# Alternating GpSimd's gathers with its table steps in an FFT-plus-ReGLU kernel

## The chip, the cores and the metric

The kernel runs on one core of one Trainium2 chip. Its time is the device time of one execution in microseconds; the number that counts is the median of the runs. The profile is of one execution, taken by the hardware profiler.

## The reference

The input x holds 8 batches of 3008 rows by 256 columns. Every batch goes through a two-dimensional FFT, of which the real part is kept; the rows that come out go through a gated feed-forward layer with 1536 inner columns.

```python
def _attn_ref(x):
    X = np.fft.fft(x, axis=1)
    X = np.fft.fft(X, axis=2)
    return X.real.astype(np.float32)

def _moe_ref(x, w_gate, w_val, w_out):
    gate = np.maximum(x @ w_gate, 0.0)
    val = x @ w_val
    return (gate * val @ w_out).astype(np.float32)

# x: (8, 3008, 256); w_gate, w_val: (256, 1536); w_out: (1536, 256)
# reference(x, ...) = _moe_ref(_attn_ref(x) as 24064 rows of 256, ...)
```

## The kernel before

**The transform.** The column transform is folded into the weights: the matrices `WA` and `WB` are the gate and value weights already multiplied by the cosine and sine tables `TA` and `TB`. The row transform is made with matmuls against two sets of tables, `tabC` and `tabS`, of which the odd columns are made during the set-up and the even columns later (below). Symmetries of the input halve and halve again the work: the rows of a batch (`XD`) and the same rows in mirrored order (`XG`) are added and subtracted ("folds"), most of it on GpSimd.

**Order of work.** The schedule is written out by hand. Each engine executes its own instructions in the order in which the program issues them, and waits on semaphores for the others. TensorE has the matmuls, ScalarE the ReLU of the gate (L814) and copies out of PSUM, VectorE the products of gate and value (`h`, L823), GpSimd the folds; SP issues most DMAs, GpSimd some.

**Batch 0** is done in four blocks (`segments`) of 376 or 377 columns, each of 12 tiles `fi`. A tile takes two gate matmuls, a ReLU, a third gate matmul (L804, the mirror half) and a second ReLU in the same PSUM bank, and the same three matmuls for the value, with two products on VectorE. The bank of the gate is one of two. Between them stand the matmuls of the second layer (L710). In the lists `more[(block, fi)]` stand steps that are slipped into a tile: the remaining weights (L380, L384) in the first eight tiles of block 0, and the steps of the even tables from tile 8 of block 0 on.

**The even tables.** For each of six columns `c` of `even_order`, `even_turns` (L430, L431) makes on GpSimd the whole number of turns of each angle, rounded, into a slice of the spare buffer `AA`. Later VectorE subtracts it from the angle (L455, `u` times `kvec` minus the slice), ScalarE takes the sine of it (L456), VectorE its absolute value (L457), and ScalarE the cosine (L458). The starting places of the six columns, counted in tiles, are

```python
EVEN_AT = (8, 10, 12, 14, 16, 17)
```

**The masking step.** Column 5 of `u`, one number per partition, is set to zero from partition 120 on. It is the lambda `u5` (L751), a VectorE instruction on 128x1 numbers that stands in tile 5 of block 0. Only L455 of column 5, the third in `even_order`, needs it; the odd tables use the copy `us`, masked in the set-up (L334).

**GpSimd's list around the change** is the function `turns_and_rows`. Ahead of it GpSimd has made the even-family folds of batch 0 (L439 to L443). Then come the turns of the six columns, with one step `minus_v` (L474, a product into the mirror operand `CB` of block 1) after the fourth, and after the turns six gathers (`load_mirror`, L117): indirect DMAs issued by GpSimd, each of which brings 128 or 120 mirrored rows of batch 1, 2 KB each, into `XG`. The next step of GpSimd is the fold of batch 1 (L150), which waits for a token `go` that VectorE writes in tile 6 of block 1 (L756) and for the gathers to land. On SP's queue the same function issues the rows of batch 1 (L94, L99, L102) and `reverse(2)` (L132), a copy of batch 2 in reversed row order from HBM to HBM.

**Later batches** are done in three blocks of 512 columns, with the sum of two parts made by L949 and L950 on VectorE and GpSimd.

Of the kernel before, what the change touches and what calls it, by code (L numbers as in the profile page):

```python
# [15 lines left out]
ALU = mybir.AluOpType  # L16
# [18 lines left out]
def kernel(  # L35
# [8 lines left out]
    nc = tc.nc  # L44
# [18 lines left out]
    def single(name, shape, dt=F32, pool=const):  # L63
        return pool.tile(shape, dt, name=name, tag=name)
# [26 lines left out]
    def load_rows(b, ts=range(3)):  # L91
        for t in ts:
            n = (128, 128, 120)[t]
            nc.sync.dma_start(out=XD[0:n, :, t].rearrange("p r a d -> p r (a d)"),  # L94
                              in_=dram(x, (b * S + 1 + t * 256) * D, [[2 * D, n], [H * D, 2], [1, 2 * D]]))

    def load_row_0(b):
        for r in range(2):
            nc.sync.dma_start(out=XD[120:121, r, 2], in_=dram(x, (b * S + r * H) * D, [[0, 1], [0, 2], [1, D]]))  # L99

    def load_mirror_0(b):
        nc.sync.dma_start(out=XG[120:121, :, 2, :, :].rearrange("p r a d -> p r (a d)"), in_=dram(x, b * S * D, [[H * D, 2], [1, 2 * D]]))  # L102
# [12 lines left out]
    def load_mirror(b, t, r):  # L115
        n = (128, 128, 120)[t]
        nc.gpsimd.indirect_dma_start(  # L117
            out=XG[0:n, r, t, :, :].rearrange("p a d -> p (a d)"), out_offset=None, in_=pairs,
            in_offset=bass.IndirectOffsetOnAxis(ap=gidx[0:n, 2 * t + r:2 * t + r + 1], axis=0), element_offset=b * S * D)
# [8 lines left out]
    def reverse(b):  # L128

        for r in range(2):  # L130
            top = (H - 1 - r * (H // 2)) - NC * PC + PC
            nc.sync.dma_start(out=xr[b, 1 - r], in_=dram(x, b * S * D + top * 2 * D, [[PC * 2 * D, NC], [-2 * D, PC], [1, 2 * D]]))  # L132
# [96 lines left out]
    pidx = single("pidx", [128, 1])  # L229
    back = single("back", [128, 1])  # L230
    u = single("u", [128, 6])
# [111 lines left out]
    nc.vector.tensor_scalar(wv[:], pidx[:], scalar1=119.0, op0=ALU.is_lt, scalar2=0.5, op1=ALU.mult)  # L343
    nc.vector.tensor_scalar(wv[:], wv[:], scalar1=0.5, op0=ALU.add, scalar2=None)

    upright = []

    def turn(r):
# [24 lines left out]
    def weights(c):  # L373

        f = slice(c * 512, (c + 1) * 512)

        def one(i, T, W):
            p = psO.tile([128, 512], F32, name="o", tag="o")
            for kc in range(2):
                nc.tensor.matmul(p[:], lhsT=T[:, kc, :], rhs=wr[i][c][:, kc, :], start=(kc == 0), stop=(kc == 1))  # L380
            if (i, c, W) == (0, 1, WA):
                return lambda: nc.scalar.copy(W[i][:, f], p[:])
            if (i, W) in ((1, WA), (c - 1, WB)):
                nc.vector.tensor_scalar(W[i][:, f], p[:], scalar1=1.0, op0=ALU.mult, scalar2=None)  # L384
            else:
                nc.scalar.copy(W[i][:, f], p[:])
        return [lambda i=i, T=T, W=W: one(i, T, W) for i in range(2) for T, W in ((TA, WA), (TB, WB))]
# [12 lines left out]
    for t in range(3):  # L400
        n = ROWS[1][t]
# [26 lines left out]
    def even_turns(n, c):  # L428
        m = spare[:, n * NE:(n + 1) * NE]
        nc.gpsimd.tensor_scalar(m, kvec[:, even_k], scalar1=us[:, c:c + 1], op0=ALU.mult, scalar2=ROUND, op1=ALU.add)  # L430
        nc.gpsimd.tensor_scalar(m, m, scalar1=-ROUND, op0=ALU.add, scalar2=float(S), op1=ALU.mult)  # L431
# [37 lines left out]
    def minus_v(e, seg):  # L469
        cols = slice(seg * NJ, seg * NJ + NJ + seg // 3)  # L470
        if e is nc.scalar:
            e.activation(VM[:, cols], V[:, cols], ACTF.Copy, scale=m2[:])
        else:
            e.tensor_scalar(VM[:, cols], V[:, cols], scalar1=m2[:], op0=ALU.mult, scalar2=0.0, op1=ALU.add)  # L474
# [5 lines left out]
    def turns_and_rows():  # L480
        load_rows(1)
        load_row_0(1)
        load_mirror_0(1)
        for n, c in enumerate(even_order):
            even_turns(n, c)
            if n == 3:
                minus_v(nc.gpsimd, 1)
        for n in range(6):
            load_mirror(1, n // 2, n % 2)
        reverse(2)  # L490


# [253 lines left out]
    CB = U  # L746
    dft_first(U, V)
    turns_and_rows()

    more = {(0, i): [s] for i, s in enumerate(weights(1) + weights(2))}  # L750
    u5 = lambda: nc.vector.scalar_tensor_tensor(u[:, 5:6], in0=pidx[:], scalar=120.0, in1=u[:, 5:6], op0=ALU.is_lt, op1=ALU.mult)  # L751
    more[(0, 5)].append(u5)
    for n, c in enumerate(even_order):
        for k, step in enumerate(even_table(n, c)):
            more.setdefault(divmod(EVEN_AT[n] + k, NF), []).append(step)
# [361 lines left out]
```

## Time and profile before

| | us |
|---|---|
| median of 3 runs | 641.34 (640.04 to 641.82) |
| the profiled execution's own time | 640.34 |
| its span, from first to last instruction | 638.6 |
| TensorE busy | 624.0 |
| VectorE busy | 554.4 |
| GpSimd busy | 506.5 |
| ScalarE busy | 449.7 |
| mean granted TensorE clock | 0.997 of full speed |

The profiled execution took 1.7 us more than its span, and 1.0 us less than the median. Busy times overlap: matmuls are pipelined, and a matmul's end is modelled, so a row of 0.32 us can be followed by the next after 0.16 us. PE is TensorE's matmuls, PEld its weight loads, DVE is VectorE, ACT ScalarE, POOL GpSimd. In timelines the columns are start, duration, engine, line, operation, output and inputs, shape and count; in brackets at the end stands the idle time before the instruction and what ended it, as inferred from semaphores.

### The profile page before, as it was taken

How to read it: one execution, taken by the hardware profiler on the slowest of the kernel's cores; microseconds unless marked ns; L12 is line 12 of the kernel's file. 1: busy time of each engine (PE TensorE's matmuls, PEld its weight loads, DVE VectorE, ACT ScalarE, POOL GpSimd, SP SyncE). 2: the span in 40 equal slices, each digit the busy share in tenths (PEclk: the TensorE clock that was granted, in tenths of full speed). 3: DMA queues.
4: the chain of work that ended last, by engine and by line, in shares of the span. 5: the costliest groups of instructions: out<-in, count | busy, mean ns of one | idle time of the engine just before them, and what ended most of it. 6: DMA issues, size and time to landing. Idle time of an engine off the chain costs nothing.

```text
span 638.6 us, 12470 instructions
## 1 busy us (share of the span) xinstructions
PE 624.0 (98%) x4098; PEld 400.5 (63%) x4145; DVE 554.4 (87%) x981; ACT 449.7 (70%) x813; POOL 506.5 (79%) x494
## 2 busy tenths in 40 slices
PE   8989999999999999999999999999999999999997
PEld 3456666566666666666666666666666666666666
DVE  7886666898999999998999899899899989999991
ACT  7667666777777777777777777777777777777752
POOL 8974993899899999798888989799896666666660
PEclk9998999999999999999999999999999999999999
DMA  9951745624273416414173324411211111211122
GB/s 239 205 191 54 188 158 156 168 95 134 78 165 124 140 67 145 148 45 146 62 196 96 124 82 101 87 52 49 76 48 50 42 58 55 57 36 51 51 58 84
DMA packets 64017, 66.38 MB, mean 104 GB/s; under 512 B 19705, under 2 KB 46905, under 8 KB 63952
## 3 DMA queue, kind: packets, MB, share of 16 engines
q1 hardware_dynamic: 59536, 60.02, 32.9%
q0 software_dynamic: 3984, 4.92, 3.8%
q8 instruction: 32, 0.52, 0.4%
q10 hardware_dynamic: 432, 0.66, 0.3%
q14 instruction: 33, 0.27, 0.1%
HBM read 41.83 MB, written 34.13 MB: 119 GB/s over the span
## 4 chain that ended last, share of the span: by engine, by line
PE 90%; DVE 5%; issue 2%; DMA 1%; POOL 1%; ACT 1%; DVEq 0%; ACTq 0%; POOLq 0%
PE o L710 36%; PE v L799 10%; PE v L804 10%; PE g L938 8%; PE p L945 8%; PE v L798 8%; PE d L527 4%; DVE h L834 3%; PE p L804 1%; DMA XG<-in_x_dram,gidx 1%; PE p L798 1%; PE p L799 1%; DVE r L949 1%; DVE h L823 1%; PE d L638 0%
## 5 line engine op out<-in xcount | busy, mean ns | idle before, releaser
L950 POOL TENSOR_TENSOR r<-r 128x512 f32<-128x512 f32 (+1 forms) x252 | 314.6, 1253 | 99.3 <-DVE r L949 98.9
L834 DVE SCALAR_TENSOR_TENSOR h<-r,v 128x512 bf16<-128x512 f32 (+1 forms) x504 | 318.6, 674 | 40.0 <-PE v L804 27.9
L710 PE MATMUL o<-wo,h 128*128 128x256 bf16 x2172 | 331.6, 273 | 0.0
L710 PEld LDWEIGHTS <-h 128*128 128x128 bf16 x2220 | 217.2, 98 | 115.2 <-issue 4.0
L933 ACT ACTIVATE p<-CB,b 128x512 f32<-128x512 bf16 (+1 forms) x252 | 172.4, 684 | 73.2 <-DVE r L949 71.7
L941 ACT COPY r<-g 128x512 f32<-128x512 f32 (+1 forms) x252 | 145.6, 578 | 66.8 <-PE g L938 59.3
L949 DVE SCALAR_TENSOR_TENSOR r<-r,p 128x512 f32<-128x512 f32 (+1 forms) x252 | 168.9, 670 | 0.6 <-ACT r L941 0.6
L799 PE MATMUL v<-V,WB 128*128 128x512 bf16 (+3 forms) x296 | 108.9, 368 | 2.3
L804 PE MATMUL v<-V,WM 128*128 128x512 bf16 (+1 forms) x252 | 94.4, 375 | 2.0 <-DVE h L834 1.6
L938 PE MATMUL g<-V,WM 128*128 128x512 bf16 (+1 forms) x252 | 94.5, 375 | 0.4 <-ACT r L941 0.3
L945 PE MATMUL p<-U,WA 128*128 128x512 bf16 (+1 forms) x252 | 94.5, 375 | 0.0
L798 PE MATMUL v<-U,WA 128*128 128x512 bf16 (+3 forms) x252 | 92.1, 366 | 0.1
L823 DVE TENSOR_TENSOR h<-r,v 128x376 bf16<-128x376 f32 (+1 forms) x88 | 45.1, 543 | 22.4 <-PE v L804 13.2
L798 PEld LDWEIGHTS <-WA 128*128 128x128 bf16 x347 | 33.9, 98 | 41.8 <-issue 13.0
L723 ACT COPY os<-o 128x512 f32<-128x512 f32 x92 | 52.5, 572 | 5.0 <-issue 4.5
L799 PEld LDWEIGHTS <-WB 128*128 128x128 bf16 x347 | 33.9, 98 | 35.1 <-DVE WB L384 1.2
L814 ACT ACTIVATE r<-p 128x376 f32<-128x376 f32 (+1 forms) x80 | 38.3, 486 | 22.0 <-PE p L804 9.3
L150 POOL TENSOR_TENSOR XG<-XG,XD 128x510 f32<-128x510 f32 x42 | 52.8, 1267 | 0.0
L158 POOL TENSOR_TENSOR AA<-XG 128x510 f32<-128x510 f32 x42 | 45.3, 1090 | 0.0
L938 PEld LDWEIGHTS <-WM 128*128 128x128 bf16 x252 | 24.7, 98 | 6.4 <-issue 1.0
L945 PEld LDWEIGHTS <-WA 128*128 128x128 bf16 x252 | 24.7, 98 | 3.4 <-issue 0.5
L804 PEld LDWEIGHTS <-WM 128*128 128x128 bf16 x252 | 24.7, 98 | 2.8
(182 smaller groups left out, 423.9 us busy)
## 6 DMA issues: line engine op xcount, KB each, us to landing
out_dram<-os SPq DMA_DIRECT2D x124, 128.0 KB
xr<-in_x_dram SPq DMA_DIRECT2D x12, 768.0 KB
XG<-xr SPq DMA_DIRECT2D x12, 768.0 KB
XD<-in_x_dram SPq DMA_DIRECT2D x15, 512.0 KB
out_dram<-os SPq DMA_DIRECT2D x35, 112.0 KB
XD<-in_x_dram SPq DMA_DIRECT2D x8, 480.0 KB
CB<-ch SPq DMA_DIRECT2D x7, 376.2 KB
out_dram<-os SPq DMA_DIRECT2D x13, 96.0 KB
```

The lines of the kernel that those rows point to most:

```text
L150: e.tensor_tensor(XG[p, r, t, ::-1, 1:D], XG[p, r, t, ::-1, 1:D], XD[p, r, t, :, D - 1:0:-1], op=ALU.add)
L710: nc.tensor.matmul(st["p"][0:m, q, :], lhsT=lhs(f), rhs=wo[:, f, :], start=(f == 0 and not (early and q)), stop=(f == NF - 1), skip_group_ ...
L798: nc.tensor.matmul(bank[:, 0:st["n"]], lhsT=WA[i][:, st["f"]], rhs=st["us"], start=True, stop=False)
L799: nc.tensor.matmul(bank[:, 0:st["n"]], lhsT=WB[i][:, st["f"]], rhs=st["vs"], start=False, stop=True)
L804: nc.tensor.matmul(bank[:, 0:st["n"]], lhsT=W[i][:, st["f"]], rhs=v, start=False, stop=True, skip_group_check=True)
L834: nc.vector.scalar_tensor_tensor(half_h(st, sign), in0=st["s"][1 + sign][:, 0:n], scalar=0.0, in1=st["v"][:, 0:n], op0=ALU.max, op1=ALU.mult)
L933: nc.scalar.activation(st["p"][:, 0:st["n"]], st["c"], ACTF.Copy, scale=b2[:, st["fi"]:st["fi"] + 1])
L938: nc.tensor.matmul(st["g"][:, 0:n], lhsT=WM[0][:, st["f"]], rhs=st["vs"], start=True, stop=True)
L941: nc.scalar.copy(q[:, 0:n], st["g"][:, 0:n])
L945: nc.tensor.matmul(st["p"][:, 0:n], lhsT=WA[0][:, st["f"]], rhs=st["us"], start=False, stop=True, skip_group_check=True)
L949: nc.vector.scalar_tensor_tensor(sp[:, 0:n], in0=q[:, 0:n], scalar=-0.5, in1=st["p"][:, 0:n], op0=ALU.mult, op1=ALU.add)
L950: nc.gpsimd.tensor_tensor(sm[:, 0:n], sp[:, 0:n], q[:, 0:n], op=ALU.add)
```

## The change

Three things are moved; no instruction is added or taken away, and neither TensorE's nor ScalarE's nor SP's list differs.

1. `minus_v` goes from behind the fourth column's turns to behind the second's.
2. Each of the first four gathers goes ahead of the turns of columns 3 to 6 in turn, so that GpSimd's list reads: turns 1, turns 2, `minus_v`, gather 1, turns 3, gather 2, turns 4, gather 3, turns 5, gather 4, turns 6, gather 5, gather 6.
3. The masking step goes from tile 5 of block 0 into the set-up, behind the two instructions that make `wv` (L343, L344) and ahead of the first folds of VectorE (L412 on).

```diff
     nc.vector.tensor_scalar(wv[:], wv[:], scalar1=0.5, op0=ALU.add, scalar2=None)
 
+    nc.vector.scalar_tensor_tensor(u[:, 5:6], in0=pidx[:], scalar=120.0, in1=u[:, 5:6], op0=ALU.is_lt, op1=ALU.mult)
     upright = []
...
         load_mirror_0(1)
         for n, c in enumerate(even_order):
             even_turns(n, c)
-            if n == 3:
+            if n == 1:
                 minus_v(nc.gpsimd, 1)
-        for n in range(6):
-            load_mirror(1, n // 2, n % 2)
+            if n:
+                load_mirror(1, (n - 1) // 2, (n - 1) % 2)
+        load_mirror(1, 2, 1)
         reverse(2)
...
     more = {(0, i): [s] for i, s in enumerate(weights(1) + weights(2))}
-    u5 = lambda: nc.vector.scalar_tensor_tensor(u[:, 5:6], in0=pidx[:], scalar=120.0, in1=u[:, 5:6], op0=ALU.is_lt, op1=ALU.mult)
-    more[(0, 5)].append(u5)
     for n, c in enumerate(even_order):
```

## The prediction

> **What bounds the kernel now.** The page comes first. The chain that ended last says which engine sets the end:
>
> ```profile
> PE 90%; DVE 5%; issue 2%; DMA 1%; POOL 1%; ACT 1%; DVEq 0%; ACTq 0%; POOLq 0%
> ```
>
> TensorE it is, so a step on another engine counts only where TensorE waits for it. The change touches the first 57 us; there I read the windows, to find where TensorE is not full, and then the timelines. Columns of a window: length, then PE, PEld, DVE, ACT and POOL busy with counts, granted clock, DMA share, GB/s.
>
> ```profile
> 33.00:38.00 5.00, 5.00 (x39) 3.68 (x38) 4.96 (x10) 3.04 (x8) 4.52 (x7) 1.00 0.39 146
> 38.00:42.50 4.50, 4.50 (x36) 3.18 (x35) 4.32 (x10) 3.99 (x10) 3.52 (x5) 1.00 0.50 192
> 42.50:47.50 5.00, 3.13 (x24) 2.20 (x23) 2.25 (x5) 2.73 (x6) 3.13 (x4) 1.00 0.78 259
> 47.50:52.50 5.00, 4.43 (x21) 2.45 (x20) 3.29 (x8) 4.21 (x10) 0.00 (x0) 0.66 0.45 143
> ```
>
> TensorE is full from 33 to 42.5; then three engines are idle together for two microseconds, and after it the clock falls to 0.66 of full. The timelines have the hole (ScalarE, TensorE, VectorE, GpSimd):
>
> ```profile
> 42.95 0.60 ACT L458 ACTIVATE tabC<-AA,half_pi 121x377 bf16<-121x377 f32 x1
> 44.71 0.48 ACT L814 ACTIVATE r<-p 128x376 f32<-128x376 f32 x1 [1.16 <-PE v L799]
> 46.23 0.48 ACT L814 ACTIVATE r<-p 128x376 f32<-128x376 f32 x1 [1.04 <-PE o L710]
> ...
> 43.12 0.32 PE L804 MATMUL p<-CB,WB 128*128 128x376 bf16 x1
> 46.76 0.32 PE L804 MATMUL p<-CB,WB 128*128 128x376 bf16 x1 [1.87 <-issue]
> ...
> 46.96 0.55 DVE L823 TENSOR_TENSOR h<-r,v 128x376 bf16<-128x376 f32 x1 [2.56 <-remote]
> ...
> 38.88 1.18 POOL L117 DMA_INDIRECT XG<-in_x_dram,gidx  x1 [0.28 <-issue]
> 45.57 0.98 POOL L117 DMA_INDIRECT XG<-in_x_dram,gidx  x1 [0.30 <-issue]
> ```
>
> The ReLU at 44.71 needs only the mirror matmul of 43.12, modelled to end at 43.44, and ScalarE was free from 43.55: it starts 1.2 late. The ReLU at 46.23 needs a matmul that ended at 44.08. TensorE's 46.76 then waits for that ReLU. The trace's record of semaphore updates says why: TensorE's increments come 0.01 behind the modelled ends until 40, but after 43.24 only at 44.69, 46.15 and 46.87, and then six of them between 47.61 and 47.81. They are held up and flushed. The stretch, 42.6 to 47.8, lies in that of the six gathers, issued back to back from 38.88 to 46.55; nowhere else in the trace does such a flush stand. Among other DMAs it does not occur: from 24 to 28 they move 300 GB/s, more than here, and nothing lags.
>
> Price of the hole: the first gate matmul of tiles 0 to 3 of block 1 starts at 38.77, 40.38, 41.99 and 43.60, 1.61 a tile; of tiles 4, 5 and 6 at 47.25, 50.51 and 54.09. Three tiles take 10.49 where 3 x 1.61 and the six transform matmuls in the third (52.93 to 54.09, 1.16) make 5.99: **4.5 us**, about 2.4 of it idle and the rest at half clock.
>
> The second place is the masking step, with VectorE and GpSimd side by side:
>
> ```profile
> 28.28 1.44 DVE L751 SCALAR_TENSOR_TENSOR u<-pidx,u 128x1 f32<-128x1 f32 x1
> 28.92 0.74 POOL L442 TENSOR_TENSOR G<-XG 121x254 bf16<-121x254 f32 x1
> 32.80 0.33 PE L799 MATMUL d<-V,WB 128*128 128x376 bf16 x1 [0.74 <-DVE WB L384]
> 33.70 0.90 DVE L455 SCALAR_TENSOR_TENSOR AA<-kvec,u,AA 128x377 f32<-128x377 f32 x1
> ```
>
> One number per partition takes 1.44 us, until GpSimd's L442 has ended at 29.66. The same form in the set-up (L334) takes 0.15.
>
> **The change part by part.** Masking step out of block 0: VectorE has no idle time from 28.28 to 34.4, so 1.4 us less lets all behind it move up. TensorE waited for VectorE twice there: 0.22 at 30.22 (a start due at 30.00) and 0.74 at 32.80. The weights of the second wait could be copied from 31.13, when their matmul ends, plus 0.68 for L384: 31.81, before the 31.89 at which TensorE wants them. So at most 0.96 comes back, at least 0.6 if VectorE is still a little behind; I take **-0.8**, near the upper row, since TensorE is full from there to 43.
>
> Masking step in the set-up: 0.15 by L334, at 6.32. VectorE idles 0.27 at 6.4 for TensorE and 1.62 ahead of 15.06 for the first mirrored rows: cost 0. Without that cover it would be 0.15. `u` is read next by L455, at 33.7.
>
> GpSimd's list: the sum of its steps is the same, so the sixth gather still issues near 45. Steps take about 1.27 a gather (38.88 to 40.36 to 41.65, gaps included) and 1.27 a column of turns. From 32.3 on: `minus_v` to 32.9, gather 1 to 34.4, third turns 35.7, fourth 38.3, fifth 40.8, sixth 43.4, gathers 5 and 6 to 46. Queued behind each gather are the turns; VectorE wants the third at 40.44 (39.6 after the gain above), the fourth at 43.80, the fifth and sixth one and two tiles later: 4 us of slack for the third and fourth, 3 or more for the others. `minus_v` is wanted at 39.89 and comes 2.5 earlier. The gathers' own waits (on GpSimd's DMAs of the set-up) are over by 20.4, and the fold that needs the data comes at 56.4. They now run beside `reverse(2)` (32 to 43.5, DMA share 0.39), whose result is not read before 71. So no cost from lateness.
>
> The hole: gathers come 2.55 apart instead of 1.27. The near row is the set-up: four gathers issued at 3.03, 5.59, 7.74 and 9.25, with data behind them, and TensorE's increments on time (two are missing from the record). I take it that spacing removes the hold. What is late next is ScalarE, which from 46.23 to 50.9 has no pause: with two table steps and two copies out (L723) between, its first ReLUs of tiles 3 and 4 lie 2.81 apart, 1.2 more than a tile. That stays: 4.5 - 1.2 gives **-3.3**; the bounds are -4.5 and 0.
>
> VectorE against GpSimd: L455 at 33.70 started inside a turn of GpSimd and took 0.90 instead of 0.60. Now turns go on until 43.4, and up to five more two-input steps (L455, L457) can meet one. A turn instruction fills about 43% of the time (1.1 of 2.55); the mean wait is half of 0.58: 8 x 0.43 x 0.29 = 1.0 on VectorE against 0.3 before. TensorE sees only what VectorE's slack (0.1 to 0.6 a tile) doesn't cover: I take **+0.2** (0 to +0.7).
>
> The Trainium skill, "SBUF — State Buffer", section "Who interferes with whom", says that a VectorE instruction with two SBUF inputs contends with a GpSimd instruction that reads SBUF, and that the second to issue blocks until the first has finished. The 1.44 and 0.90 agree; it speaks against spreading the turns. With each of the eight steps blocked for a whole turn, 8 x 0.58 would be 4.6 on VectorE, an estimate at its limit.
>
> Sum: -0.8 - 3.3 + 0.2 = **-3.9**. The profiled execution's 640.34 becomes 636.4; the median stands 1.0 above it, so 641.34 becomes 637.4.
>
> **The rivals.** *The hole stays as it is.* It may have to do with something else in that stretch: TensorE's instruction fetch lies in it (16 KB at 45.86), and the DMA share is 0.78. For: I can show a coincidence only. Against: the other 31 such fetches have no flush, nor has 24 to 28. Then -0.8 + 0.2 is left: 640.7. The Trainium skill states in the same section that "DMA never contends with a compute engine"; by it the gathers' data could not hold TensorE up, and the time would be that of this rival. The trace shows the coincidence, which speaks against it without settling it.
>
> *Every gather in flight holds TensorE's increments, however spaced.* The four gathers from 41.65 on cost 4.5, 1.1 each; the stretch now lasts from 33.2 to 46 and covers a part where TensorE is full, so six isolated holds cost 6.7 instead of 4.5, +2.2, and a second stretch of half clock like that of 48.7 to 52.1 costs 1.7: -0.6 + 2.2 + 1.7 = +3.3, 644.6 (from 642.9 without the second). It decides if the hold begins as soon as the first gather's data move (three microseconds after issue). For: two increments missing at 4.05 and 8.76, each inside a gather of the set-up. Against: the first two gathers of batch 1 pass without lag.
>
> *The change does not do what it says:* the order of instructions shows it does; no chance.
>
> **How the numbers follow.** This kernel's runs differ by about 0.3% (1.92), which I use as the bound of no change: 639.42 and 643.26. Forecast 0.53, with a range of its own from 635.9 (-0.96 - 4.5) to 639.0 (-0.6 - 2.4 + 0.7, a quarter of the hold staying). Hole stays: 0.25, 640.4 to 641.4. Holds multiply: 0.22, 642.9 to 646, a little of it under the bound. Faster 0.53, same 0.26, slower 0.21. The range of 635.9 to 643.2 takes in the first two and the foot of the third.
>
> **What would show it.** In the profile after: the masking step (now L346) at 0.15 in the set-up; no 1.44 on VectorE; no wait of 0.74 at L799 near 32. The gathers alternate from 33 to 46, and ScalarE's L814 has no gap of 1 us there; tiles 3 to 6 of block 1 take about 7.2 instead of 10.5, at clock 1.0. I am wrong if increments of TensorE come in a flush again, if a clock of 0.5 stands between 35 and 55, or if L455 or L457 are long and TensorE waits for VectorE.

## The result, and the profile after

The changed kernel takes **636.43 us** (median of 4 runs, 636.23 to 636.55), the kernel before beside it 641.02 (4 runs, 640.04 to 641.82): a ratio of 0.9929, 95% interval 0.9912 to 0.9946. The profiled executions took 640.34 and 636.55, with spans of 638.6 and 634.8. The forecast was 637.4, by way of 640.34 to 636.4 for the profiled execution.

The chain that ended last, after, is TensorE's still:

```profile
PE 91%; DVE 5%; issue 2%; ACT 1%; DVEq 0%; ACTq 0%
```

The windows after (columns as before: length, PE, PEld, DVE, ACT, POOL, clock, DMA share, GB/s):

```profile
33.00:38.00 5.00, 5.00 (x39) 3.68 (x38) 4.67 (x10) 3.52 (x9) 4.40 (x5) 1.00 0.49 179
38.00:42.50 4.50, 4.50 (x35) 3.14 (x34) 4.26 (x10) 3.91 (x10) 3.98 (x5) 1.00 0.55 200
42.50:47.50 5.00, 4.33 (x32) 2.93 (x31) 4.20 (x9) 4.78 (x12) 4.01 (x5) 1.00 0.63 195
47.50:52.50 5.00, 5.00 (x36) 3.02 (x34) 3.87 (x9) 4.10 (x11) 0.28 (x1) 1.00 0.56 171
```

In the third window TensorE has 4.33 instead of 3.13, ScalarE 4.78 of 5.00 instead of 2.73, and in the fourth the clock is 1.00 instead of 0.66. The timelines after, at the places shown of before:

```profile
6.24 0.15 DVE L346 SCALAR_TENSOR_TENSOR u<-pidx,u 128x1 f32<-128x1 f32 x1
...
32.32 0.33 PE L799 MATMUL d<-V,WB 128*128 128x376 bf16 x1 [0.21 <-DVE WB L385]
...
43.18 0.92 DVE L456 SCALAR_TENSOR_TENSOR AA<-kvec,u,AA 128x377 f32<-128x377 f32 x1
...
43.70 0.48 ACT L814 ACTIVATE r<-p 128x376 f32<-128x376 f32 x1 [0.22 <-PE p L799]
45.36 1.07 ACT L725 COPY os<-o 128x512 f32<-128x512 f32 x2
46.30 0.51 ACT L814 ACTIVATE r<-p 128x376 f32<-128x376 f32 x1
...
46.86 0.32 PE L804 MATMUL p<-CB,WB 128*128 128x376 bf16 x1 [0.39 <-ACT r L814]
...
33.40 1.39 POOL L117 DMA_INDIRECT XG<-in_x_dram,gidx  x1 [0.17 <-issue]
34.82 1.00 POOL L431 TENSOR_SCALAR AA<-kvec,us 128x377 f32<-128x377 f32 x1
46.80 0.99 POOL L117 DMA_INDIRECT XG<-in_x_dram,gidx  x1 [0.31 <-issue]
```

The masking step is a row of 0.15 in the set-up. L799 waits 0.21 where it waited 0.74. The gathers alternate with turns from 33.40 to 47.79; the first five start 2.7 to 3.3 apart (forecast 2.55), the sixth 1.35 behind the fifth. From 34 on no ReLU there has a gap of 1 us ahead of it (1.13 stands ahead of the one at 33.82, which waits for its own matmuls, as one at 34.30 did before with 1.79). The one at 46.30 is late because ScalarE itself is full. In the trace's record of semaphore updates, 5 of TensorE's 56 are missing between 33 and 52, but those that are there come within 0.1 of the modelled ends of the matmuls, and no flush stands.

### The profile page after: what moved, and what is told of

Its sections match the earlier page's. It is cut to its first block, busy times and chain, and to the rows that moved or that the text cites. A ratio compares the mean times of both kernels' runs of the same rounds, so it can differ in the third digit from the quotient of the medians.

```text
span 634.8 us, 12470 instructions
## 1 busy us (share of the span) xinstructions
PE 622.9 (98%) x4098; PEld 400.3 (63%) x4145; DVE 553.0 (87%) x981; ACT 449.1 (71%) x813; POOL 507.1 (80%) x494
## 4 chain that ended last, share of the span: by engine, by line
PE 91%; DVE 5%; issue 2%; ACT 1%; DVEq 0%; ACTq 0%
PE o L712 36%; PE v L799 10%; PE v L804 10%; PE g L938 8%; PE p L945 8%; PE v L798 7%; PE d L529 4%; DVE h L834 3%; PE p L804 1%; PE p L798 1%; PE p L799 1%; DVE r L949 1%; PE v L351 1%; DVE h L823 1%; PE d L640 0%
## 5 line engine op out<-in xcount | busy, mean ns | idle before, releaser
L799 PE MATMUL v<-V,WB 128*128 128x512 bf16 (+3 forms) x296 | 108.6, 367 | 2.3
L725 ACT COPY os<-o 128x512 f32<-128x512 f32 x92 | 52.5, 572 | 5.0 <-issue 4.5
L799 PEld LDWEIGHTS <-WB 128*128 128x128 bf16 x347 | 33.8, 97 | 34.1 <-DVE WB L385 0.6
```

Of the source, the lines that this page charges most:

```text
L799: nc.tensor.matmul(bank[:, 0:st["n"]], lhsT=WB[i][:, st["f"]], rhs=st["vs"], start=False, stop=True)
```

## The experiments

All line numbers move by one or a few between kernels. "Tile 3 to 6" is the time from the first gate matmul of tile 3 of block 1 to that of tile 6: 10.49 before, 7.11 after.

### First four kernels: each half alone, and the burst in other forms

e1 moves only the masking step; e2 moves only the gathers; e3 moves the masking step and puts the burst of six gathers behind the fourth column's turns, some 3 us earlier; e4 moves the masking step and replaces the six gathers, in their old place, by plain GpSimd DMAs.

```diff
 e3:         if n == 3:
                 minus_v(nc.gpsimd, 1)
+                for k in range(6):
+                    load_mirror(1, k // 2, k % 2)
-        for n in range(6):
-            load_mirror(1, n // 2, n % 2)
 e4:     for n in range(6):
-            load_mirror(1, n // 2, n % 2)
+            plain_mirror(1, n // 2, n % 2, nc.gpsimd)   # dma_start of 128 or 120 rows, 2 KB each
```

> Only the masking step moves; the six gathers stay back to back behind the turns. If the hole comes from the burst of gathers: the hole stays in its place (three tiles from the first gate matmul of tile 3 of block 1 take about 10.5 us, TensorE increments late between 42 and 48), the 1.44 us instruction and the 0.74 us wait near 32 are gone, and the time is 0.5 to 0.9 below the kernel before, ratio 0.9986 to 0.9992. If moving the masking step had removed the hole (by shifting TensorE against the gathers): three tiles near 7.2 and 4 us less.

> Only the gathers alternate with the turns; the masking step stays in tile 5 of block 0. If the burst makes the hole: no late increments, three tiles near 7.1 us, the 1.44 us instruction still there; 3.4 to 4.5 below the kernel before, ratio 0.993 to 0.9947. If the hole has another cause in that stretch (an instruction fetch, the DMA load): three tiles near 10.5, ratio 1.000.

> Masking step in the set-up; the six gathers stay back to back, but behind the fourth turns instead of the sixth, about 3.3 us earlier (35.6 to 43.3 instead of 38.9 to 46.5). If the burst makes the hole, it comes about 3.3 us earlier with it (late increments from about 39 to 44.5, in tiles 1 and 2 of block 1), and the time is that of the masking step alone, ratio 0.997 to 1.0. If the hole belongs to a place in TensorE's program or to its instruction fetch, it stays at tile 3.

> Masking step in the set-up; in the place of the six gathers six plain DMAs of the same size, also issued back to back by GpSimd, which bring the rows of batch 1 in forward order (so batch 1 of the output is not the reference's). If any burst of GpSimd-issued DMAs of 256 KB makes the hole: as in the run with the masking step alone. If the indirect form makes it: no late increments, three tiles near 7.2 us, ratio 0.992 to 0.995.

| | median (lowest to highest) | ratio to before, interval | tile 3 to 6 |
|---|---|---|---|
| the kernel before, 31 runs | 636.68 (636.16 to 637.54) | | |
| e1 | 636.49 (636.12 to 636.73) | 0.9995, 0.9985 to 1.0005 | 7.12 |
| e2 | 636.77 (636.33 to 637.43) | 1.0003, 0.9994 to 1.0013 | 7.11 |
| e3 | 636.31 (636.05 to 636.64) | 0.9997, 0.9987 to 1.0006 | 7.11 |
| e4 | 636.55 (636.18 to 636.79) | 0.9997, 0.9987 to 1.0006 | 7.11 |

Here the kernel before itself took 636.68, not 641, and every kernel with a burst was without the hole. e1's burst is the burst of before, and its increments are on time. e3's burst, which comes with a higher DMA share than e1's, passes too (windows of e3):

```profile
38.00:42.50 4.50, 4.50 (x36) 3.19 (x34) 4.27 (x10) 4.00 (x9) 3.58 (x4) 1.00 0.71 262
42.50:47.50 5.00, 4.32 (x32) 2.87 (x30) 4.17 (x8) 4.78 (x12) 3.74 (x6) 1.00 0.81 277
```

TensorE has the 4.32 of a kernel without a hole at a DMA share of 0.81, above the 0.78 of the hole in the first profile of before and equal to the 0.81 of the hole in e5 below. No theory had foreseen this. So the load on the DMA engines does not make the hole by itself, and a burst of gathers does so only at some times. These four kernels could not tell the theories apart, because there was nothing to remove.

### The kernel before once more

e5 is the kernel before, unchanged, at another time on the same chip number.

> The kernel before, once more, with a profile. If the hole belongs to the kernel's order on every chip, it is there again (tiles 3 to 6 of block 1 in 10.5 us, span near 638.6). If it belongs to the chip or the session of the first runs, as the times of the kernel before beside the first four experiments suggest (636.7 instead of 641), tiles 3 to 6 take 7.1 us, all increments are on time, the records of the gathers' semaphores are complete, and the span is near 635; the masking step takes between 0.15 and 1.44 us, by where GpSimd stands at that moment.

It took 639.77 (638.47 to 640.83), the kernel before beside it 640.07 (637.43 to 641.23). The hole was back, in the same place (windows of e5):

```profile
42.50:47.50 5.00, 3.52 (x24) 2.16 (x23) 2.80 (x6) 2.70 (x7) 3.36 (x4) 1.00 0.81 257
47.50:52.50 5.00, 3.90 (x17) 2.25 (x17) 2.48 (x5) 3.87 (x9) 0.00 (x0) 0.66 0.50 157
```

One semaphore counts all of TensorE's increments, so they can be matched with its matmuls in order. Here they were up to 2.6 late (up to 3.0 in the first profile of before: the matmul of L799 that ended at 44.57 has its increment at 47.61). Five came together from 47.87 on, and the clock was at half for 3.41 from 48.53. The same code on the same chip number takes 636.7 at one time and 640 at another. There is no profile of the kernel before without the hole, but behind this stretch kernels with and without it agree: from the token `go` to the end it is 582.32 in the first profile of the kernel before, 582.27 in e5, 582.35 in e1, 582.37 after.

### The same kernels where the hole is present

e6, e7 and e8 are e2, e3 and e4 again; e9 issues the six plain DMAs from SP, behind `reverse(2)`. The kernel before took 639.27 beside them (31 runs, 636.60 to 641.36, 22 of them over 638.5), so it had its hole in most runs.

> Only the gathers alternate, once more, since the hole of the kernel before comes at some times and not at others (636.7 beside the first four experiments, 640.1 beside the fifth run, same chip number). If the kernel before is slow beside this run (over 638.5): alternating removes the hole, three tiles 7.1 us, 636.3 to 637.4; if the hole does not come from the burst of gathers, this kernel is as slow as the one before. If the kernel before is fast beside it, both are equal and nothing is told apart.

> Masking step in the set-up, six gathers back to back 3.3 us earlier. Where the kernel before has the hole: if the burst makes it, late TensorE increments from about 39 to 44.5 and a time of 638.5 to 640.5; if a place in TensorE's program or its instruction fetch makes it, the hole stays at 43 to 48. Where the kernel before has none: 636.3.

> Masking step in the set-up, six plain DMAs issued back to back by GpSimd in place of the gathers (forward order of rows, so batch 1 of the output is not the reference's). Where the kernel before has the hole: if any burst of DMAs that GpSimd issues makes it, it is there, 638.5 to 640.5; if the indirect form makes it, 636.4. Where it has none: 636.5.

> Masking step in the set-up, six plain DMAs of the same rows issued by SP, behind the copy of batch 2, in place of the gathers (forward order, so batch 1 of the output is not the reference's). Where the kernel before has the hole: if the load on the DMA engines makes it, a hole stands where these DMAs run (from about 32); if issuing from GpSimd makes it, no hole, 636.3 to 636.6. Where it has none: 636.5.

| | median (lowest to highest) | ratio to before, interval | tile 3 to 6 |
|---|---|---|---|
| e6, gathers spaced | 636.23 (636.12 to 637.20) | 0.9959, 0.9939 to 0.9978 | 7.11 |
| e7, burst earlier | 637.82 (636.61 to 638.97) | 0.9973, 0.9955 to 0.9991 | 8.95 |
| e8, plain DMAs by GpSimd | 636.36 (635.97 to 636.60) | 0.9954, 0.9936 to 0.9972 | 7.12 |
| e9, plain DMAs by SP | 635.93 (635.62 to 636.16) | 0.9948, 0.9931 to 0.9964 | 7.12 |

e7 has the hole, and its end comes earlier. Its windows, a ReLU that starts late, TensorE's matmul that waits for ReLUs, and the last gather of the burst:

```profile
42.50:47.50 5.00, 3.12 (x22) 1.96 (x21) 2.93 (x7) 3.01 (x8) 4.08 (x6) 1.00 0.67 243
47.50:52.50 5.00, 4.52 (x30) 2.61 (x30) 3.20 (x7) 4.10 (x11) 0.00 (x0) 1.00 0.33 105
...
45.31 0.48 ACT L813 ACTIVATE r<-p 128x376 f32<-128x376 f32 x1 [1.06 <-PE o L711]
...
45.84 0.32 PE L803 MATMUL p<-CB,WB 128*128 128x376 bf16 x1 [1.67 <-ACT r L813]
...
43.34 1.06 POOL L117 DMA_INDIRECT XG<-in_x_dram,gidx  x1 [0.30 <-issue]
```

The burst was moved forward by 2.2 to 2.9 (its first gather issues at 36.35, against 38.88 in the first profile of before and 39.27 in e5, its last at 43.34, against 45.57 and 45.80), and the flush that ends the hole came forward with it: four increments from 45.23 on, against 47.61 to 47.81 before and from 47.87 in e5. In all three it begins 0.8 to 1.1 after the issue of the last gather has ended (44.40, 46.55 and 46.78).

The start of the hole moved by 0.7 to 0.9 only. The first ReLU that is held up starts at 43.77 in e7, 44.71 before and 44.34 in e5, for matmuls that ended at 42.73, 43.44 and 43.61. The expectation had late increments from about 39 on, but nothing was late during the first four gathers of e7, nor during the first three of before and e5. So the end of the burst sets the end of the hole. What sets its start, the burst or a place in TensorE's program, is not shown. Such a place alone is not enough, since e6 and e11 have the same list on TensorE and no hole.

TensorE's instruction fetch, which the first rival suspected, is not it: the 16 KB come at 45.11 in e7, when increments have been late since 42.7, and at 45.18 in e3 and 45.69 in e8, which have no hole. The hole costs less there (8.95 against 7.11, so 1.84) and no half clock follows.

e8 issues the same bytes from the same engine, in 3.35 instead of 7.7 (a row of GpSimd's timeline and a window; the last row is a window of e9, whose plain DMAs SP issues):

```profile
38.74 3.35 POOL L123 DMA_DIRECT2D XG<-in_x_dram  x6
...
42.50:47.50 5.00, 4.32 (x31) 2.85 (x30) 3.89 (x8) 4.78 (x12) 0.00 (x0) 1.00 0.79 273
...
38.00:42.50 4.50, 4.50 (x35) 3.14 (x34) 4.35 (x10) 3.92 (x10) 1.10 (x2) 1.00 0.93 328
```

There is no hole in either, and e8's record of updates has no gap there. So bytes into `XG`, GpSimd as the issuer and the share of the DMA engines (0.93 in e9) are not enough. It takes the indirect form, or what came with it here: an issue that lasts 7.7 instead of 3.35, and the reversed order of rows. These were not tested apart. e6 shows that the spacing alone removes it, with no help from the masking step. e7 was the least clear in time: its runs overlap with those of the kernel before, and its median lies under the expected 638.5 to 640.5, since its hole is smaller. That it has the hole rests on its profile.

### A better version, and the changed kernel once more

What is left between tiles 4 and 5 after the change (44.74 to 47.35, 2.61 instead of 1.61) was put down to ScalarE. The expectation of e10 calls them tiles 3 and 4; here they are counted as in the prediction. e10 takes two steps from ScalarE and has GpSimd make them behind the sixth gather; e11 is the changed kernel as it is.

```diff
-            steps += [lambda tab=tab: act(tab[r, 5, even_k], tab[r, 5, even_k], ACTF.Copy, scale=wv[r])
+            steps += [lambda tab=tab: nc.gpsimd.tensor_scalar(tab[r, 5, even_k], tab[r, 5, even_k], scalar1=wv[r],
+                                                              op0=ALU.mult, scalar2=0.0, op1=ALU.add)
                       for tab in (tabS, tabC)]
```

> The changed kernel, in which the two masking steps of column 5's even tables (L461, a product with wv into tabS and tabC) are made by GpSimd, behind its sixth gather, and no longer by ScalarE; the output is the reference's. In the profile after, ScalarE has no pause from 44.6 to 50.3 and TensorE's first gate matmul of tile 4 comes 2.61 after that of tile 3, instead of 1.61. Theory (ScalarE's queue is what is late there): 1.2 us less on ScalarE (0.60 + 0.64), so tile 4 comes about 1.6 to 1.9 after tile 3, GpSimd does the two steps between 46 and 49 and the d matmul at 49.7 does not wait; time 0.7 to 1.0 under the changed kernel beside it. Rival (what is left in tiles 3 and 4 is a held increment of the gathers, not ScalarE): tile 4 still comes 2.6 after tile 3, no gain. Against the kernel before: 3.5 to 5.5 us less if it has its hole in these runs, 0.7 to 1.0 if it has not.

> The changed kernel once more, unchanged, beside the kernel before in the same runs. Theory (six gathers back to back hold TensorE's increments at some times, spaced ones never): 636.2 to 636.9 whatever the kernel before does; where that has its hole it takes 640 to 641, where it has not 636.5 to 636.9. Rival (the difference belongs to the chip and not to the gathers' spacing): the changed kernel also shows runs of 640 and more.

The kernel before took 640.30 beside them (11 runs, 638.27 to 641.85). e11 took 636.33 (636.17 to 636.61), ratio 0.9941, 0.9925 to 0.9957, with tile 3 to 6 at 7.12. **e10 took 635.78** (635.65 to 636.01), ratio 0.9933, 0.9917 to 0.9949: faster than both kernels, 0.55 below e11, and their runs don't overlap. GpSimd's and ScalarE's timelines of e10, and a window:

```profile
47.40 0.59 POOL L461 TENSOR_SCALAR tabS<-tabS,wv 121x377 bf16<-121x377 bf16 x1
47.98 0.57 POOL L461 TENSOR_SCALAR tabC<-tabC,wv 121x377 bf16<-121x377 bf16 x1
...
44.57 1.07 ACT L725 COPY os<-o 128x512 f32<-128x512 f32 x2
45.51 0.52 ACT L814 ACTIVATE r<-p 128x376 f32<-128x376 f32 x1
...
42.50:47.50 5.00, 4.61 (x35) 3.13 (x33) 4.38 (x9) 4.55 (x11) 4.22 (x6) 1.00 0.65 208
```

The second table is ready at 48.55 and is read from 48.75 on. Tile 5 comes 2.24 after tile 4 instead of 2.61, and tile 6 2.77 after tile 5 instead of 2.90: 0.50 together. The direction was right; the sizes were not, since 1.6 to 1.9 were expected for the first and 0.7 to 1.0 for the gain. The pair of copies out (L725, 1.07) still stands ahead of a ReLU without a pause between them; whether it makes what is left was not tested.

## Why the prediction was right, point by point

- **TensorE sets the end, and the gain lies in two places.** It does. From the first tile of block 0 to the first second-layer matmul it took 13.39 before and 12.50 after; tile 3 to 6 went from 10.49 to 7.11; from `go` on nothing differs by more than 0.05.
- **Masking step out of block 0, -0.8 (-0.96 to -0.6).** 13.39 to 12.50 is -0.89 between these two executions. But the 1.44 was this execution's: in e5, e2 and e6 the same step in the same place takes 0.70, 0.70 and 0.69, and the stretch 12.64, 12.64 and 12.63, so in these three moving it is worth 0.14. The last section shows the difference. The term was sized right for its profile and too large for the kernel.
- **Masking step in the set-up, 0.** It took 0.15, and its place cannot be seen in the time: e1 has 12.50 in block 0 and the median is 0.2 under before where nothing else differs.
- **Lateness of the turns, 0.** TensorE is full from 33 to 42.5 in the windows after. The sixth gather issues at 46.80, 1.8 later than the "near 45" of the forecast, its last rows land at 51.45, and the fold that needs them starts at 52.71.
- **The hole, -3.3: a gain of 4.5 less 1.2 that ScalarE keeps.** 10.49 less 7.11 is -3.38. ScalarE's remainder is 7.11 less the 5.99 without limits, 1.12; e10 shows that 0.50 of it is ScalarE's, and the rest was not tested. e6, e7, e8 and e11 show the cause that could only be argued as a coincidence: gathers issued back to back, at times when the condition below is present.
- **VectorE against GpSimd, +0.2 (0 to +0.7).** It came out at 0: of L456 and L458 one was long (the row at 43.18, 0.92 instead of 0.60) and TensorE did not wait for it.
- **The sum.** -0.89 and -3.38 make -4.27; the spans differ by -3.8. The first tile of block 0 starts 0.41 later after (19.99 against 19.58), which accounts for most of the rest. It is not the change's: over all thirteen profiles this start lies between 19.51 and 20.05, and e11, the same kernel, has 19.65. Nor does it follow the clock: full clock came at 10.57 after and at 7.77 before, but e9 has it at 8.03 and starts at 20.01. The medians differ by 4.6, since the profiled execution of before lay 0.7 under the median of its runs and that of after 0.1 above. That -3.9 and -3.8 lie so close is in part luck: the terms came out 0.37 better than forecast, and the late start took that back.

**The rivals.** "The hole stays" fell: it went, in the result, in e6 and in e11, in 20 runs of spaced gathers beside a kernel before that had it in most of its runs, none of the 20 above 637.20. "Every gather holds increments, however spaced" fell by the same runs. The Trainium skill, "SBUF — State Buffer", section "Who interferes with whom", was quoted with "DMA never contends with a compute engine". For the engine itself the traces agree, since in the hole a matmul still takes its 0.32; but the report of its end comes late, up to 3.0 before and 2.6 in e5, and the page's rule did not cover that.

**What the forecast did not see** is that the hole belongs to a condition outside the kernel. Three runs of the kernel before, all with it, looked like a fixed price, and that it was present again beside the result was luck. Where the condition is absent, the halves of the change are worth nothing that can be measured: e1 0.9995 and e2 1.0003. The whole change was not run there. What the condition is stays open. It is not the chip number, since e1 to e5 have one, and not the program, since e5 is the kernel before.

The condition leaves a mark in a single profile. The landing of a gather is told by 16 semaphore updates, so the first five gathers of batch 1 make 80. e1, e2 and e3 have all 80 on record. The profiles with the hole have 22 (before), 20 (e5) and 36 (e7), and those with spaced gathers beside a kernel before that had it 54 (after), 59 (e6), 61 (e10) and 57 (e11). So the mark stands in the very executions in which spacing kept the hole away. That records go missing where increments come late suggests a rival that was not tested: the recording itself may take part. Every run timed here has a span and a clock on record, so none shows the kernel without recording.

## What to carry to other kernels

Where several engines stop together and then several semaphore updates arrive at once, ask which transfers are being issued in that stretch, and space them among other work of the same queue; it costs nothing if their data are not wanted yet. A gain that comes from removing such a stall should be measured at more than one time, because the kernel before may not have it every time. A long duration of a short instruction in one profile (1.44 for 128 numbers) should be looked up in a second profile before it becomes a term of a sum.

## What the runs showed of the hardware

**Gathers and semaphores.** Six indirect DMAs issued by GpSimd back to back, 128 or 120 rows of 2 KB each, can delay TensorE's semaphore increments by up to 3.0 us (before; 2.6 in e5) until several arrive together. They did so in before, e5 and e7, and did not in e1 and e3. Five of them spaced by 2.7 to 3.4 did not in any of five profiles, and plain DMAs of the same size from GpSimd (e4, e8) or SP (e9) did not either. How the gathers reach TensorE's updates was not shown.

**VectorE behind GpSimd.** The masking step of e6, beside the GpSimd steps around it:

```profile
28.21 0.69 DVE L752 SCALAR_TENSOR_TENSOR u<-pidx,u 128x1 f32<-128x1 f32 x1
28.16 0.73 POOL L441 TENSOR_TENSOR F<-XG 121x256 bf16<-121x256 f32 x1
28.84 0.73 POOL L442 TENSOR_TENSOR G<-XG 121x254 bf16<-121x254 f32 x1
```

Here the step ends at 28.90, as L441 does (28.89). Before, L441 ended at 28.99, but the step lasted until 29.72, through the whole of L442, which started 0.64 later than it. So 0.69 is the wait for one GpSimd step and 1.44 for two, of which the second had started after the VectorE step. What decides between the two is not shown.

**The clock.** Full clock came between 7.58 and 10.57 after the start, whatever the kernel, and half clock lasted 3.41 both in the profile before and in e5. The Trainium skill, "TensorE: Matmul & The Clock Gate", section "What's actually happening", says that activity is watched in a free-running window of about 3.4 us, so that the number of matmuls at the low clock differs from run to run. Both agree with it. e7's smaller hole was followed by no half clock at all.
